# Decode attention on one core: the PE's attention as one 8-round loop, with fixed DMA slots and the output projection behind all of PV

## The chip, the cores and the metric

One core of one Trainium2 chip. The metric is device microseconds of one execution; the spans in the profiles are about 1.8 us shorter than these times (429.7 against 431.48 us in the kernel before), because they begin and end with the kernel's own instructions. The engines go by the profile's names: PE for the matrix products (PEld for its weight loads), DVE, ACT and POOL for the other arithmetic, and SP, which issues the DMAs. QK and PV are the two products of attention, of the queries with K and of the softmax weights with V. Ratios are computed as the mean time of one kernel's fast runs over that of the other's fast runs of the same rounds, so they are not quite the ratio of the medians that are quoted.

## The reference, cut to what matters

Two tokens (batch 2, one query position each) pass through a modulated layernorm, grouped attention over a cache of 32,768 keys, an output projection, and an MLP.

```python
B, Sq, D = (2, 1, 1024)
Hq, Hkv, Sk, Dh = (32, 4, 32768, 128)      # 8 query heads share one K/V head
mod = (_silu(c) @ w_mod)                    # 12.6 MB of weights
h = _layernorm(x) * (1 + ca) + sa
q = h @ wq                                  # 8.4 MB
p = softmax(q @ k_cache^T * Dh**-0.5)       # 67 MB of K
o = p @ v_cache                             # 67 MB of V
x = x + ga * (o @ wo)                       # 8.4 MB
x = x + gb * MLP(modulated layernorm(x))    # w1, w2: 14.7 MB
```

In all 178 MB are read once, for a few matrix products with two columns. There are 2 x 4 = 8 pairs of batch and K/V head; one pair is called a round below. A round reads 4 chunks of K and 4 chunks of V of 2 MB each.

## The kernel before

Everything large goes through one SBUF arena of 160 KB per partition, by DMAs that the SP issues in the order of a list, each as soon as the PE has released the bytes that it overwrites. Before, the arena is a ring of any item sizes, so ten 2 MB chunks fit.

```python
KT_sb = [sb(f"KT_sb{i}", [128, 8, 128], BF16) for i in range(NKT)]     # NKT = 6
arena = nc.alloc_sbuf_tensor("arena", [128, RING], mybir.dt.uint8)     # RING = 160 * 1024
abase = nc.lookup_mloc(arena).addr
...
for n in range(NK + VLAG):                          # NK = 32 chunks, VLAG = 5
    if n < NK:
        add(("K", n), [TPC, D], kv_src(A_k_cache, n // NCH, n % NCH))
    v = n - VLAG
    if v >= 0:
        add(("V", v), [TPC, D], kv_src(A_v_cache, v // NCH, v % NCH))
        if v % (2 * NCH) == 2 * NCH - 1:            # after every second round
            add(("wo", g), [8, DM], ...)
```

The PE transposes a K chunk in 8 groups of 8 tiles, the DVE and the ACT copy the transposed tiles to SBUF, the PE multiplies them with the 8 query columns, and, a softmax later, it multiplies the weights with V. All of this is straight-line code: each of the 8 rounds is written out, and each wait compares a semaphore with a constant.

```python
for n in range(NK + VLAG + 1):
    for g8 in range(TPC // 8):
        if n < NK:
            ...                                      # 8 transposes, one copy of 128x1024
            pipe.append((n, g8, kn))
        if pipe and (len(pipe) > PIPE or n >= NK):
            qk(*pipe.pop(0))                         # 8 matmuls of 8 columns
        for fn in later.get((n, g8), ()):            # softmax, extract, wo
            fn()
    if 0 <= n - VLAG < NK:
        pv(n - VLAG)                                 # 16 matmuls of 512 columns
```

## Time and profile before

| | before |
|---|---|
| time, median of 3 runs | 431.48 us (431.33 to 431.48) |
| span in the profile | 429.7 us |
| data packets (queue q1), share of 16 DMA engines' span | 97.6% |
| instruction packets (queue q8) | 47 of 16 KB, 0.6% |
| PE busy | 292.2 us (68%) |
| duration of a 16 KB data packet, read from the trace's DMA records | 611 ns |

The first lines are from the page of the kernel before: busy time by engine, the bytes a second in 40 slices of the span, the DMA queues (packets, MB, share of 16 engines' span), the shares of the chain that ended last, and two lines of the DMA issues (count, KB each, median us to landing).

```profile
PE 292.2 (68%) x6035; PEld 258.2 (60%) x6035; DVE 162.5 (38%) x344; ACT 158.9 (37%) x266; POOL 1.3 (0%) x9
...
GB/s 332 432 422 426 433 432 424 432 424 427 427 432 427 426 433 429 427 433 426 426 432 426 430 433 424 429 432 426 429 429 428 430 429 424 435 424 424 427 386 112
...
q1 hardware_dynamic: 14112, 178.27, 97.6%
q8 instruction: 47, 0.77, 0.6%
...
DMA 70%; PE 24%; ACT 2%; DVE 2%; issue 1%; SPq 1%; ACTq 0%
...
K<-in_A_k_cache_dram SPq DMA_DIRECT2D x32, 2048.0 KB, 44.2
V<-in_A_v_cache_dram SPq DMA_DIRECT2D x32, 2048.0 KB, 43.2
```

The DMA is the limit: nothing dips between the first slice and the last two (422 to 435 GB/s), and a chunk lands 44 us after its issue, which is about the time that nine others ahead of it in the queue take (9 x 2.1 MB at 428 GB/s, an estimate). The PE is off the critical path for most of the run (24% of the chain, the DMA 70%). But q8 is worth a look: the page lists packets of the program itself among those of the DMA engines, 47 of them, and in the trace's DMA records 46 of the 47 overlap a data packet that takes over 150 ns longer than others of its size.

The second view is the table by stretches of the same kernel, for the last 14 us. Its columns are the stretch, its length, busy us (and instructions) of PE, weight load, DVE, ACT and POOL, the granted clock (as a share of the PE's full clock), the DMA share, and GB/s.

```profile
412.00:414.00 2.00, 0.76 (x28) 0.77 (x29) 0.22 (x1) 0.00 (x0) 0.00 (x0) 0.50 1.02 426
...
416.00:418.00 2.00, 0.00 (x0) 0.00 (x0) 0.00 (x0) 0.00 (x0) 0.00 (x0) 0.50 0.76 315
418.00:420.00 2.00, 1.84 (x64) 1.79 (x64) 0.00 (x0) 0.00 (x0) 0.00 (x0) 0.50 0.51 209
420.00:422.00 2.00, 0.03 (x2) 0.00 (x0) 0.00 (x0) 0.00 (x0) 0.00 (x0) 0.50 0.52 221
422.00:424.00 2.00, 0.69 (x26) 0.70 (x27) 0.00 (x0) 0.00 (x0) 0.00 (x0) 0.50 0.46 193
424.00:426.00 2.00, 1.44 (x55) 1.36 (x52) 0.00 (x0) 0.00 (x0) 0.00 (x0) 0.50 0.21 78
```

The reader should look at the DMA share. It falls to one half at about 417 us and stays there for 6 us, the half-busy tail below: eight of the sixteen engines, by that share, have nothing left to do (the trace's DMA records have 16 data packets under way at 414 us and 8 at 420 us), while the other eight still carry pieces of the last weights, for which the kernel must wait (the chain's last DMA, of `w`, lands at 425.7 us).

Third, the PE's timeline at about 75 us, where the PE has data and no wait (start, us, engine, line, operation; in brackets the idle time before and its cause):

```profile
74.97 0.24 PE L441 MATMUL psS<-qT,KT_sb 128*128 128x8 bf16 x4
76.08 0.26 PE L441 MATMUL psS<-qT,KT_sb 128*128 128x8 bf16 x4 [0.87 <-issue]
```

The PE stands still for 0.87 us in the middle of eight equal matmuls, for nothing that the profile shows. The trace's DMA records have an instruction packet that starts at 73.8 us and takes 0.88 us. Such packets come about once per 256 PE instructions (47 for 12,070 matmuls and weight loads); the 256 instructions of one packet are called a page below.

### The profile page before, as it was taken

Reading aid. Unit: us, or ns where it says so; the run is one execution under the profiler, and the core shown is the slowest. Engines: PE = TensorE matmul, PEld = TensorE weight load, DVE = VectorE, ACT = ScalarE, POOL = GpSimd, SP = SyncE. Lnnn points to the kernel's source line nnn. Section 1 sums busy time; section 2 is a strip of 40 time slices with the busy share of each in tenths; the row PEclk is TensorE's granted clock in tenths of the full one; section 3 lists DMA queues with packets and bytes.
Section 4 is the critical chain, followed back from the end, with each engine's and each line's share of the span. In section 5 each row is a group of like instructions: output and inputs, shape, how many; then the busy total and the mean of one; then the engine's idle time right before and its main releaser. Section 6 shows DMA issues by size and latency. Waiting matters only on the chain.

```text
span 429.7 us, 12974 instructions
## 1 busy us (share of the span) xinstructions
PE 292.2 (68%) x6035; PEld 258.2 (60%) x6035; DVE 162.5 (38%) x344; ACT 158.9 (37%) x266; POOL 1.3 (0%) x9
## 2 busy tenths in 40 slices
PE   0643379859978764997877649777777697535553
PEld 0632379858867663896757548667666585203543
DVE  0200027545665332463543435445434454203200
ACT  1100016575574325362833534446436343500100
POOL 1000000000000000000000000000000000000000
PEclk9999999998989867696996959986988599555555
DMA  8999999999999999999999999999999999999992
GB/s 332 432 422 426 433 432 424 432 424 427 427 432 427 426 433 429 427 433 426 426 432 426 430 433 424 429 432 426 429 429 428 430 429 424 435 424 424 427 386 112
DMA packets 14500, 179.11 MB, mean 417 GB/s; under 512 B 1767, under 2 KB 1774, under 8 KB 2798
## 3 DMA queue, kind: packets, MB, share of 16 engines
q1 hardware_dynamic: 14112, 178.27, 97.6%
q8 instruction: 47, 0.77, 0.6%
q10 hardware_dynamic: 334, 0.02, 0.1%
q14 instruction: 7, 0.06, 0.0%
HBM read 178.28 MB, written 0.00 MB: 415 GB/s over the span
## 4 chain that ended last, share of the span: by engine, by line
DMA 70%; PE 24%; ACT 2%; DVE 2%; issue 1%; SPq 1%; ACTq 0%
DMA K<-in_A_k_cache_dram 50%; PE psKT L546 15%; DMA V<-in_A_v_cache_dram 9%; DMA w<-in_B_w_dram 7%; DMA wmod<-in_w_mod_dram 5%; PE psS L441 4%; PE psO L473 2%; PE psM L510 1%; ACT E_sb L462 1%; SPq L344 1%; PE psM L494 0%; DVE KT_sb L552 0%; PE psM L483 0%; ACT L462 0%; DVE msum L488 0%
## 5 line engine op out<-in xcount | busy, mean ns | idle before, releaser
L546 PE MATMUL psKT<-ident,K 128*128 128x128 bf16 x2048 | 181.1, 240 | 55.1 <-DMA K<-in_A_k_cache_dram 54.2
L546 PEld LDWEIGHTS psKT<-ident,K 128*128 128x128 bf16 x2048 | 138.2, 108 | 70.0 <-DMA K<-in_A_k_cache_dram 63.5
L550 ACT ACTIVATE KT_sb<-psKT 128x1024 bf16<-128x1024 bf16 x96 | 98.3, 1024 | 190.2 <-PE psKT L546 181.3
L552 DVE COPY KT_sb<-psKT 128x1024 bf16<-128x1024 bf16 x160 | 108.2, 689 | 137.7 <-PE psKT L546 137.0
L441 PE MATMUL psS<-qT,KT_sb 128*128 128x8 bf16 x2048 | 91.6, 168 | 7.2 <-ACT KT_sb L550 4.5
L441 PEld LDWEIGHTS psS<-qT,KT_sb 128*128 128x128 bf16 x2048 | 84.0, 100 | 8.6 <-ACT KT_sb L550 4.9
L473 PE MATMUL psO<-V,E_sb 128*32 128x512 bf16 x512 | 38.2, 424 | 10.1 <-DMA V<-in_A_v_cache_dram 9.5
L462 ACT ACTIVATE E_sb<-S_sb,negm 128x256 bf16<-128x256 f32 x64 | 32.5, 508 | 7.0 <-DVE negm L460 5.2
L447 DVE TENSOR_REDUCE m1c<-S_sb 128x8 f32<-128x512 f32 x32 | 22.0, 688 | 14.1 <-ACT S_sb L446 13.0
L473 PEld LDWEIGHTS psO<-V,E_sb 128*32 128x32 bf16 x512 | 11.5, 101 | 22.3 <-DMA V<-in_A_v_cache_dram 13.3
L446 ACT ACTIVATE S_sb<-psS 128x512 f32<-128x512 f32 x32 | 19.0, 594 | 4.4 <-PE psS L441 4.3
L418 PE MATMUL psS<-siluT,wmod 128*128 128x2 bf16 x384 | 11.2, 165 | 8.4 <-DMA wmod<-in_w_mod_dram 6.9
L418 PEld LDWEIGHTS psS<-siluT,wmod 128*128 128x128 bf16 x384 | 10.9, 104 | 8.8 <-DMA wmod<-in_w_mod_dram 7.3
L426 PE MATMUL psS<-hT,wq 128*128 128x2 bf16 x256 | 7.5, 165 | 12.5 <-DMA wq<-in_A_wq_dram 12.5
L426 PEld LDWEIGHTS psS<-hT,wq 128*128 128x128 bf16 x256 | 7.1, 104 | 12.8 <-DMA wq<-in_A_wq_dram 12.8
L591 PE MATMUL psS<-gT,w 128*128 128x2 bf16 x224 | 6.6, 165 | 9.2 <-DMA w<-in_B_w_dram 9.2
L395 ACT ACTIVATE stat<-stat 128x2 f32<-128x2 f32 x3 | 0.6, 203 | 31.8 <-DVE stat L394 31.8
L591 PEld LDWEIGHTS psS<-gT,w 128*128 128x128 bf16 x224 | 6.3, 104 | 9.5 <-DMA w<-in_B_w_dram 9.5
L462 ACT ACTIVATION_READ_ACCUMULATOR E_sb<-S_sb,negm 128x1 f32 x64 | 12.0, 187 | 0.0
L485 DVE RECIPROCAL rinv<-psM 128x1 f32<-128x1 f32 x8 | 1.3, 168 | 22.1 <-PE psM L483 22.1
L573 PE MATMUL psS<-h2T,w 128*128 128x2 bf16 x224 | 7.8, 172 | 2.5 <-DVE x1b L577 1.3
L573 PEld LDWEIGHTS psS<-h2T,w 128*128 128x128 bf16 x224 | 7.6, 118 | 2.6 <-issue 2.6
(86 smaller groups left out, 93.3 us busy)
## 6 DMA issues: line engine op xcount, KB each, us to landing
K<-in_A_k_cache_dram SPq DMA_DIRECT2D x32, 2048.0 KB, 44.2
V<-in_A_v_cache_dram SPq DMA_DIRECT2D x32, 2048.0 KB, 43.2
wmod<-in_w_mod_dram SPq DMA_DIRECT2D x8, 1536.0 KB, 17.2
wq<-in_A_wq_dram SPq DMA_DIRECT2D x4, 2048.0 KB, 37.7
wo<-in_A_wo_dram SPq DMA_DIRECT2D x4, 2048.0 KB, 43.0
w<-in_B_w_dram SPq DMA_DIRECT2D x4, 1792.0 KB, 41.8
w<-in_B_w_dram SPq DMA_DIRECT2D x3, 2048.0 KB, 31.0
w<-in_B_w_dram SPq DMA_DIRECT2D x1, 1024.0 KB, 29.4
```

The costliest lines, as they stand in the source:

```text
L418: pe(lambda e, w=it.view, j=j, k=k: e.matmul(psS[0][:, 2 * j:2 * j + 2], lhsT=w[:, j * 128:(j + 1) * 128], rhs=siluT[:, :, k], start=(k == ...
L426: pe(lambda e, w=it.view, h=h, k=k: e.matmul(psS[1][:, 2 * h:2 * h + 2], lhsT=w[:, k % 2, h * 128:(h + 1) * 128], rhs=hT[:, k, :], start=( ...
L441: pe(lambda e, t=t, jj=jj: e.matmul(ps[:, t * HPG:(t + 1) * HPG], lhsT=KT_sb[kn][:, jj, :], rhs=qT[:, b, g * HPG:(g + 1) * HPG], start=Tru ...
L446: act(lambda e: e.activation(Sc, ps[:, :].rearrange("p (t h) -> p h t", h=HPG), ACT.Copy), reads=[preg], writes=[f"S_sb{i % 2}_{cc}"])
L447: dve(lambda e: e.tensor_reduce(m1c[:, :, cc], Sc, AX.X, ALU.max), reads=[f"S_sb{i % 2}_{cc}"], writes=[f"m1c{cc}"])
L462: act(lambda e, h=h: e.activation(E_sb[j][:, :, h, :], S_sb[j][:, h, :].rearrange("p (u t) -> p u t", t=4), ACT.Exp, bias=negm[j][:, h:h + ...
L473: pe(lambda e, t4=t4, tg=tg, q=q: e.matmul(psO[32 * q:32 * q + 32, :], lhsT=E_sb[j][:, tg // 4, :, :].rearrange("p h t -> p (h t)"), rhs=i ...
L546: pe(lambda e, kq=kq, jj=jj, w=it.view, t=t: e.transpose(psKT[kq][:, jj * 128:(jj + 1) * 128], w[:, t, :], ident[:, :]), reads=[it.reg, "i ...
L550: act(lambda e, kn=kn, src=src: e.activation(KT_sb[kn][:, :, :], src, ACT.Copy), reads=[f"psKT{kq}"], writes=[f"KT_sb{kn}"])
L552: dve(lambda e, kn=kn, src=src: e.tensor_copy(KT_sb[kn][:, :, :], src), reads=[f"psKT{kq}"], writes=[f"KT_sb{kn}"])
L573: pe(lambda e, w=it.view, fc=fc, q=q, j=j, k=k: e.matmul(psS[0][:, 2 * fc:2 * fc + 2], lhsT=w[:, k % 2, q * 512 + j:(q + 1) * 512:4], rhs= ...
L591: pe(lambda e, w=it.view, q=q, j=j, k=k: e.matmul(psS[1][:, 2 * k:2 * k + 2], lhsT=w[:, q % 2, j * DM + k * 128:j * DM + (k + 1) * 128], r ...
```

## The change

The intent: the 8 rounds become one loop on the PE, whose body is about 1,200 instructions (256 transposes, 256 QK and 64 PV matmuls, each with its weight load, are 1,152; the rest are small matmuls, branches and register operations). For that, every K and V chunk gets a fixed slot (8 slots of 16 KB instead of a ring), each producer gets a semaphore of its own that counts rounds, and the PE's waits compare with a register. The other engines' code stays straight-line. The query columns of a round are copied by the POOL to one place, E_sb and two small tiles exist once instead of twice, the copies of K have 8 buffers instead of 6, and the output projection of all four groups moves behind the last PV. The core of the diff, cut:

```diff
-VLAG = 5
-NKT = 6
+NKT = 8
...
+    def _loop(self, eng, body, bounds):
+        with eng.Fori(*bounds) as it:
+            val = {(1, 0): it}
+            for scale, off in ((1, -1), (16, 0), (16, -1)):
+                val[scale, off] = eng.snap(it * scale + off * scale)
+            for always, ops in body:
+                ...                                  # the waits: wait_ge(sem, val[scale, off])
+                if always:
+                    run()
+                else:
+                    with eng.If(it > bounds[0]):     # what lags one round behind
+                        run()
...
-    atT = [sb(f"atT{i}", [128, 8, 2], BF16) for i in range(2)]
+    qcur = sb("qcur", [128, HPG], BF16)
+    atT = [sb(f"atT{i}", [128, 8, 2], BF16) for i in range(G)]
-    yacc = sb("yacc", [128, KT8, 2])
...
-    negm = [sb(f"negm{i}", [128, HPG]) for i in range(2)]
-    rowsum = [sb(f"rowsum{i}", [128, HPG]) for i in range(2)]
+    negm = sb("negm", [128, HPG])
+    rowsum = sb("rowsum", [128, HPG])
-    E_sb = [sb(f"E_sb{i}", [128, NT // 4, HPG, 4], BF16) for i in range(2)]
+    E_sb = sb("E_sb", [128, NT // 4, HPG, 4], BF16)
...
+    SLOT = {("K", 0): 0, ("K", 1): 1, ("V", 0): 2, ("V", 1): 3, ("K", 2): 4, ("V", 2): 5, ("K", 3): 6, ("V", 3): 7}
...
+    T.fold(rounds)
...
+    for g in range(G):
+        it = need("wo", g)
+        ...                                          # wo, all four groups, into one PSUM tile
```

## The prediction

> **What bounds the kernel now.** The DMA. The page's slices show the 16 engines 90% busy or more from start to the last slice, at 420 to 435 GB/s, the chain of waits 70% DMA. The PE has slack: when it catches up (75 to 86 us, the timeline) a K chunk takes 6.2 us, or with its PV also 6.2 us, so about 25 us a round, while a round's 16.8 MB need about 39 us of DMA. There is no hole in the DMA until 416 us; then, in the table by stretches, the DMA share falls to 0.5 from 418 to 423 us and to 0.4 until 425; the last landing is at 425.7. Half of the engines end 7 to 8 us before the other half, and the last `w2` pieces wait for these.
>
> **Why half are late.** The page's queue list shows queue q8, kind instruction: 47 packets of 16 KB, 0.6% of 16 engines' span. The packets' times in the trace are spread over the whole run, about one for each 256 PE instructions, and their durations (0.88 to 0.97 us) repeat with period 8, so I read 8 of the 16 engines in turn, about 6 each. 7 us over 6 pages is about 1.2 us a page: the late half is late because it feeds the PE its program (estimate). At page ends the PE stops for 0.87 us about 1.4 us after the packet began, so pages are fetched nearly on demand and not far ahead.
>
> **What the change does.** Bytes of data, matmuls, evacuations and exps are the same. The ring shrinks from 10 slots to 8; stream order equals PE order, so 7 slots, about 34 us, stay queued: no DMA hole. Output projection (4 x 1.8 us of PE) moves behind PV, under the landing of wo, w1, w2. The PE's program becomes about 1,300 instructions ahead, a body of about 1,250, and 1,650 behind: 17 pages instead of 47, if the body stays on chip. [...] No loop in this trace decides. [...] I give 70% that the body stays.
>
> - Body stays: 28 to 30 pages fewer, 3.5 to 3.7 per late engine x about 1.2 us = about 4.3 us from the DMA's end, all on the critical path: 427.
> - Body is fetched each round: 50 to 60 pages[...]: 432 to 433.
>
> [...]
>
> **Prediction:** 427.6 us, 8 in 10 between 425.5 and 433. Faster by over 2%: 0.05; within: 0.90; slower: 0.05.
>
> **What would show it.** q8 packets about 17 to 25 (body stays) or 50 and more; the DMA share's half-busy tail 3 to 4 us instead of 8; DMA share 1.0 and GB/s unchanged before; PE busy hardly changed; last landing at about 421.5 us.
>
> **What would make it wrong.** Back edges or Ifs that cost many us and push a round's PE time over 39 us: the K stretches would then wait for the PE and the DMA share fall. A slot that comes free late (8 instead of 10) and leaves DMA holes. The late half late for another reason than pages.

How the number comes about: 431.5 us of the kernel before, less about 4.3 us, is about 427 if the body stays, and 432 to 433 if it is fetched each round; 427.6 lies a little above the first.

## The result, and the profile after

| | before | after |
|---|---|---|
| time, median of 4 runs each | 431.46 us | 430.73 us (430.44 to 430.87) |
| ratio | | 0.9983 (0.9969 to 0.9997) |
| span in the profile | 429.7 us | 429.0 us |
| instruction packets (q8) | 47 | 16 |
| duration of a 16 KB data packet, mean of the undisturbed ones | 611.0 ns | 615.6 ns |
| the same for 8 KB and 7 KB packets | 309.0, 272.0 ns | 314.8, 277.2 ns |

The kernel was to gain about 3.9 us and gained 0.7. The same lines of the page of the kernel after:

```profile
PE 289.7 (68%) x6035; PEld 253.2 (59%) x6035; DVE 162.9 (38%) x340; ACT 155.0 (36%) x266; POOL 2.8 (1%) x17
...
GB/s 330 428 418 418 428 419 429 422 424 425 428 428 428 428 428 425 428 428 428 427 428 428 428 425 429 426 429 425 429 426 427 428 428 427 428 424 412 419 416 155
...
q1 hardware_dynamic: 14112, 178.27, 98.4%
q8 instruction: 16, 0.26, 0.2%
...
DMA 79%; PE 17%; ACT 1%; SPq 1%; DVE 1%; issue 1%; DVEq 0%; ACTq 0%
...
K<-in_A_k_cache_dram SPq DMA_DIRECT2D x32, 2048.0 KB, 32.2
V<-in_A_v_cache_dram SPq DMA_DIRECT2D x32, 2048.0 KB, 35.7
```

And the last stretches:

```profile
416.00:418.00 2.00, 0.35 (x13) 0.36 (x14) 0.00 (x0) 0.00 (x0) 0.00 (x0) 0.50 0.99 410
418.00:420.00 2.00, 1.52 (x57) 1.43 (x54) 0.00 (x0) 0.00 (x0) 0.00 (x0) 0.50 1.03 430
420.00:422.00 2.00, 0.00 (x0) 0.00 (x0) 0.00 (x0) 0.00 (x0) 0.00 (x0) 0.50 0.73 295
422.00:424.00 2.00, 1.38 (x52) 1.39 (x52) 0.00 (x0) 0.00 (x0) 0.00 (x0) 0.50 0.39 156
424.00:426.00 2.00, 1.38 (x51) 1.29 (x47) 0.00 (x0) 0.00 (x0) 0.00 (x0) 0.50 0.01 4
```

Half of what was foreseen is there. The body is not fetched again: after the first round there is no instruction packet from 91.5 to 380 us, 16 are left of 47, and the half-busy tail shrinks from about 8 us to about 3. But the tail did not become shorter by ending earlier. It became shorter because the early half now ends at 420.5 us instead of 416.7. The engines were slower in the mean over the run, and the DMA share shows no gap (1.01 from 80 to 380 us in both): q1's packets take 98.4% of 429.0 us (422.1 us an engine) against 97.6% of 429.7 (419.4), though they carry the same 178.27 MB and are less disturbed (16 instruction packets, not 47). Where no instruction packet comes at all, in slices 11 to 34, the rate is an even 425 to 429 GB/s, no better than before with its packets; outside of the loop, where data packets are 7 to 12 KB, it falls to 412 to 419 in five slices (a sixth of 419, slice 6, already carries 16 KB packets).

The DMA records say how. Most data packets take 3 to 11 ns longer, and about as much at 7 KB as at 16 KB (in the mean 5.2 ns at 7 KB, 5.8 at 8, 3.2 at 12, 4.6 at 16): more like a fixed addition to each packet than one in step with its size. Over the 12,672 large packets, 8,704 x 4.6 + 1,024 x 3.2 + 1,920 x 5.8 + 1,024 x 5.2 ns = 60 us, or 3.7 us for each of 16 engines. That is about the size of what was missing. A fixed addition for each packet points to something that every packet shares, and the sizes, the sources and the queue are the same.

What had changed was the address. The tensors ahead of the arena changed in size: KT_sb by +4,096 bytes a partition, E_sb by -4,096, atT by +64, yacc by -64, negm and rowsum by -32 each, qcur by +32 (16 bytes, rounded up). Together that is -32. When both kernels are built, the arena starts at byte 61440 before and at 61408 after: 61440 is a multiple of 256, 61408 lies 224 past one. That the address is the cause, and that 256 bytes are the step that counts, was the guess, which neither of the two traces showed. It was for the chip to say.

### The profile page after: what moved, and what is told of

Same layout as the page of the kernel before. It is cut to its first block, busy times and chain, and to the rows that moved or that the text cites. A ratio compares the mean times of both kernels' runs of the same rounds, so it can differ in the third digit from the quotient of the medians.

```text
span 429.0 us, 13364 instructions
## 1 busy us (share of the span) xinstructions
PE 289.7 (68%) x6035; PEld 253.2 (59%) x6035; DVE 162.9 (38%) x340; ACT 155.0 (36%) x266; POOL 2.8 (1%) x17
## 3 DMA queue, kind: packets, MB, share of 16 engines
q1 hardware_dynamic: 14112, 178.27, 98.4%
## 4 chain that ended last, share of the span: by engine, by line
DMA 79%; PE 17%; ACT 1%; SPq 1%; DVE 1%; issue 1%; DVEq 0%; ACTq 0%
DMA K<-in_A_k_cache_dram 59%; PE psKT L476 11%; DMA wo<-in_A_wo_dram 8%; DMA w<-in_B_w_dram 7%; DMA wmod<-in_w_mod_dram 5%; PE psS L488 3%; PE psO L518 1%; SPq L373 1%; ACT KT_sb L480 1%; PE psS L612 0%; ACT E_sb L509 0%; PE psO L646 0%; ACT L509 0%; DVE KT_sb L482 0%; PE psM L422 0%
## 5 line engine op out<-in xcount | busy, mean ns | idle before, releaser
L476 PE MATMUL psKT<-ident,K 128*128 128x128 bf16 x2048 | 175.2, 238 | 42.5 <-DMA K<-in_A_k_cache_dram 42.5
L476 PEld LDWEIGHTS psKT<-ident,K 128*128 128x128 bf16 x2048 | 134.3, 106 | 52.8 <-DMA K<-in_A_k_cache_dram 49.3
L488 PE MATMUL psS<-qcur,KT_sb 128*128 128x8 bf16 x2048 | 88.8, 168 | 9.8 <-ACT KT_sb L480 7.1
L488 PEld LDWEIGHTS psS<-qcur,KT_sb 128*128 128x128 bf16 x2048 | 80.1, 99 | 15.5 <-ACT KT_sb L480 9.4
L455 PE MATMUL psO<-hT,wq 128*128 128x2 bf16 x256 | 7.5, 165 | 12.9 <-DMA wq<-in_A_wq_dram 12.9
L612 PE MATMUL psS<-atT,wo 128*128 128x2 bf16 x256 | 7.5, 165 | 12.4 <-DMA wo<-in_A_wo_dram 12.4
L612 PEld LDWEIGHTS psS<-atT,wo 128*128 128x128 bf16 x256 | 7.1, 104 | 13.3 <-DMA wo<-in_A_wo_dram 13.3
L455 PEld LDWEIGHTS psO<-hT,wq 128*128 128x128 bf16 x256 | 7.1, 104 | 13.2 <-DMA wq<-in_A_wq_dram 13.2
L646 PE MATMUL psO<-gT,w 128*128 128x2 bf16 x224 | 6.6, 165 | 9.8 <-DMA w<-in_B_w_dram 9.8
L646 PEld LDWEIGHTS psO<-gT,w 128*128 128x128 bf16 x224 | 6.3, 104 | 10.1 <-DMA w<-in_B_w_dram 10.1
```

Of the source, the lines that this page charges most:

```text
L455: pe(lambda e, w=it.view, h=h, k=k: e.matmul(psO[:, 2 * h:2 * h + 2], lhsT=w[:, k % 2, h * 128:(h + 1) * 128], rhs=hT[:, k, :], start=(k = ...
L476: pe(lambda e, kq=kq, jj=jj, w=it.view, t=t: e.transpose(psKT[kq][:, jj * 128:(jj + 1) * 128], w[:, t, :], ident[:, :]), reads=[it.reg, "i ...
L488: pe(lambda e, t=t, jj=jj: e.matmul(ps[:, t * HPG:(t + 1) * HPG], lhsT=KT_sb[g8][:, jj, :], rhs=qcur[:, :], start=True, stop=True), reads= ...
L612: pe(lambda e, w=it.view, g=g, j=j, k=k: e.matmul(psS[0][:, 2 * k:2 * k + 2], lhsT=w[:, j, k * 128:(k + 1) * 128], rhs=atT[g][:, j, :], st ...
L646: pe(lambda e, w=it.view, q=q, j=j, k=k: e.matmul(psO[:, 2 * k:2 * k + 2], lhsT=w[:, q % 2, j * DM + k * 128:j * DM + (k + 1) * 128], rhs= ...
```

## The experiments

Theory A: two effects of equal size cancel, a gain from 31 instruction packets fewer and a loss from the arena's address. Rival B: the loop gains little, because the DMA's rate falls for another reason (8 slots, another order of the stream, another core). Theory A has two halves, which the first three runs take apart. All runs gave correct results. Unless said otherwise, one set of runs shares the kernel before on its chip: 431.39 us in the first set, of which one run of 538.6 us is left out.

### The kernel after, with the arena back on its old address

```diff
+    sb("pad", [128, 8])
     arena = nc.alloc_sbuf_tensor("arena", [128, RING], mybir.dt.uint8)
```

> The kernel after, with 32 bytes of padding ahead of the DMA arena, so that it starts at byte 61440 of each partition as before, and not at 61408 (224 past a multiple of 256). Theory A (the start address): 16 KB data packets go back from 612 to 621 ns to a flat 611, 8 KB ones from 313 to 320 to 309; about 12,700 packets over 16 engines at 4 to 6 ns each are 3.9 us an engine, so 426.8 us (426 to 427.8), last landing at about 421. Rival B (the order of the stream, 8 slots in place of 10, or the core that was profiled): nothing changes, 430.7 us and packets of 612 to 621 ns. Instruction packets: 16 in both.

Measured: 426.17 us (425.94 to 426.33), ratio to before 0.9879 (0.9864 to 0.9895), 16 instruction packets, 16 KB packets of 611.0 ns, 8 KB 309.0. The last stretches:

```profile
414.00:416.00 2.00, 0.99 (x38) 0.91 (x35) 0.00 (x0) 0.00 (x0) 0.00 (x0) 0.50 1.03 434
416.00:418.00 2.00, 0.00 (x0) 0.00 (x0) 0.00 (x0) 0.00 (x0) 0.00 (x0) 0.50 0.73 299
418.00:420.00 2.00, 1.87 (x64) 1.79 (x64) 0.00 (x0) 0.00 (x0) 0.00 (x0) 0.50 0.33 139
420.00:422.00 2.00, 1.02 (x33) 0.94 (x33) 0.41 (x2) 0.00 (x0) 0.00 (x0) 0.50 0.04 8
```

Here the early half ends where it did before (the share drops in 416 to 418), and the late half ends 5 to 6 us earlier than before. Three stretches of the middle make the same point; they are of the kernel before, the kernel after and this one, in this order:

```profile
20.00:40.00 20.00, 8.21 (x279) 7.73 (x276) 0.78 (x4) 0.00 (x0) 0.00 (x0) 1.00 1.01 425
80.00:380.00 300.00, 227.29 (x4397) 198.77 (x4393) 137.51 (x265) 142.24 (x245) 0.00 (x0) 0.84 1.01 428
```

```profile
20.00:40.00 20.00, 7.96 (x269) 7.48 (x267) 0.78 (x4) 0.00 (x0) 0.00 (x0) 1.00 1.01 418
80.00:380.00 300.00, 228.08 (x4366) 193.98 (x4363) 141.78 (x271) 140.12 (x247) 1.32 (x7) 0.87 1.01 427
```

```profile
20.00:40.00 20.00, 8.27 (x281) 7.79 (x279) 0.78 (x4) 0.00 (x0) 0.00 (x0) 1.00 1.01 426
80.00:380.00 300.00, 232.01 (x4423) 198.57 (x4419) 141.81 (x271) 139.69 (x247) 1.33 (x7) 0.85 1.01 431
```

With a DMA share of 1.01 in all six, the DMA was never idle; only its rate differs. 32 bytes of padding are worth 4.6 us. Rival B falls, its slower core included: the arena at 61504, below, ran on the same chip as this one and took 429.92 us.

### The kernel before, with the arena moved off its address

```diff
+    sb("pad", [128, 120])        # 480 bytes: the arena starts at 61920, 224 past a multiple of 256
     arena = nc.alloc_sbuf_tensor("arena", [128, RING], mybir.dt.uint8)
```

> The kernel before, with the arena moved by 480 bytes to 61920 (224 past a multiple of 256, as after). Theory A: packets of 612 to 621 ns, 47 instruction packets as before, both delays add up: 431.4 + 3.9 = about 435.3 us (434 to 436.5). Rival B: 431.4 us and packets of 611 ns.

Measured: 436.23 us (436.15 to 436.25), ratio 1.0113 (1.0097 to 1.0129); 47 instruction packets, 16 KB packets of 615.6 ns, 8 KB of 314.8, the very means of the kernel after. The address costs 4.8 us in the kernel before as well, a little more than expected. So it has nothing to do with the loop, the slots or the order. The sum of 3.7 us over the data packets does not give all of the 4.6 to 4.8. A part may be that the instruction packets take longer too: 1.07 us in the mean here and 1.06 in the kernel after, against 0.94 in both aligned kernels, which for 47 packets on 8 engines is 0.75 us (estimate). The rest stays open.

### The aligned kernel after, with its rounds written out

```diff
     sb("pad", [128, 8])
...
-        self.ops["pe"].append(("loop", [], body, (first, max(rounds) + 1)))
+        for it in sorted(rounds):
+            for always, ops in rounds[it]:
+                self.ops["pe"].extend(ops)
```

> The aligned kernel after with its 8 rounds written out again for the PE (same slots, semaphores, order of the stream, output projection behind PV; no loop, no If, waits on constants). If the gain of the loop is the instruction packets that are not fetched: 46 to 48 such packets, half-busy tail of 7 to 8 us again, 431.4 us (430.7 to 432.2), as the kernel before. If slots, order or the projection matter by themselves: a time apart from 431.4 with 47 packets. If packets of instructions cost nothing: the time of the aligned loop.

Measured: 431.55 us (431.34 to 431.60), ratio 1.0003 (0.9989 to 1.0018). 47 instruction packets, and the half-busy tail is back:

```profile
416.00:418.00 2.00, 0.00 (x0) 0.00 (x0) 0.00 (x0) 0.00 (x0) 0.00 (x0) 0.50 0.71 291
418.00:420.00 2.00, 1.52 (x57) 1.52 (x58) 0.00 (x0) 0.00 (x0) 0.00 (x0) 0.50 0.60 254
420.00:422.00 2.00, 0.34 (x13) 0.26 (x10) 0.00 (x0) 0.00 (x0) 0.00 (x0) 0.50 0.47 201
422.00:424.00 2.00, 0.62 (x23) 0.63 (x24) 0.00 (x0) 0.00 (x0) 0.00 (x0) 0.50 0.54 217
424.00:426.00 2.00, 1.42 (x53) 1.33 (x51) 0.00 (x0) 0.00 (x0) 0.00 (x0) 0.50 0.18 74
```

So fixed slots, 8 in place of 10, the new order, the projection behind PV, the semaphores and the padding together are worth nothing, for better or worse: 431.55 against 431.39. All of the gain is in the loop. The four corners:

| | arena on a multiple of 256 | arena 224 past one |
|---|---|---|
| rounds written out, 47 instruction packets | 431.4 (before), 431.55 (after, unrolled) | 436.23 (before, moved) |
| rounds in a loop, 16 instruction packets | 426.17 | 430.73 (after) |

The loop gains 5.4 us on the left (5.2 counted from the kernel before) and 5.5 on the right; the address costs 4.6 to 4.8.

### How round the address has to be

The kernel after with the arena at 61504 (64 past a multiple of 256), at 61568 (128 past), and at 61696 (a multiple of 256, not of 512). The edit is the size of the pad: 24, 40 and 72 elements instead of 8.

> The kernel after with the arena at 61504: a multiple of 64 but 64 past a multiple of 256. If a start off a multiple of 256 is what costs[...]: packets of 612 to 621 ns and 430.7 us still. If a multiple of 64 is enough: 611 ns and 426.8 us.

> The loop with the arena at 61568, 128 past a multiple of 256. If only multiples of 256 are free of the extra time: 16 KB packets of about 614 to 615 ns and about 430 us, as at 64 past. If 128 is enough: 611 ns and 426.2 us.

> The loop with the arena at 61696, a multiple of 256 but not of 512 or 4096. If a multiple of 256 is what the data packets need: 611 ns for 16 KB and 426.2 us. If only a coarser boundary (512, 4096) helps: longer packets and 429 to 431 us.

| start past a multiple of 256 | 16 KB packet, mean | time | median of before in the same set |
|---|---|---|---|
| 0 (61440) | 611.0 ns | 426.17 | 431.39 |
| 0 (61696) | 611.0 ns | 426.05 | 431.32 |
| 64 (61504) | 614.7 ns | 429.92 | 431.39 |
| 128 (61568) | 614.6 ns | 429.77 | 431.43 |
| 224 (61408) | 615.6 ns | 430.73 | 431.46 |

In these five places, a multiple of 256 is enough, and neither 64 nor 128 past one is. The price at 224 past (615.6 ns, 430.73 us) is a little higher than at 64 and 128 (614.7 and 614.6 ns, 429.92 and 429.77 us).

### Does the body really stay, and in how much room?

Two rounds in one body of the aligned loop: 4 iterations of about 2,400 instructions. (The first case of the expectation supposes that the room for the body is smaller than this one.)

```diff
-        with eng.Fori(*bounds) as it:
+        with eng.Fori(1, 5) as it:
+            for half in range(2):                  # round 2 * it - 1 + half
...
-                    with eng.If(it > bounds[0]):
+                        with eng.If(it > 1):        # in the first half alone
```

> The aligned loop with two rounds in one body: 4 iterations of about 2,520 PE instructions, 9.8 pages of 256[...]. If the loop gains because its body stays on chip[...]: every iteration fetches its body again, about 50 instruction packets and 431 to 432.5 us, as without a loop. If the room is larger or the loop gains for another reason (fewer waits, registers): about 21 packets and 427 us.

Measured: 432.64 us (432.62 to 432.94), ratio 1.0033 (1.002 to 1.0046), 53 instruction packets, spread evenly over all four iterations:

```profile
q8 instruction: 53, 0.87, 0.7%
```

A loop with a body of about 4.7 pages of 256 instructions fetched it once (no packet from 91.5 to 380 us in the kernel after); one of twice that size fetched it anew in every iteration (53 packets), and was slower than no loop at all (432.64 against 431.55 us). So it isn't the loop that gains, it is that the body is not fetched again. What differs between the two is the size of the body, so the room for it should lie between about 4.7 and 9.4 pages (an estimate from these two runs); where in between was not shown.

### What one page costs: two misses and a clean dose

To see a page's price apart from the loop, two runs added PE instructions without data. First, the unrolled aligned kernel with every QK matmul issued twice:

```diff
-        for jj in range(8):
+        for k in range(16):
+            jj = k % 8
```

> The unrolled aligned kernel with every QK matmul issued twice (same values to the same place): 4,096 more PE instructions, 16 more pages, no more data; about 6 us more PE work a round, which fits into the PE's slack of about 14 us. If an instruction page costs one of 8 DMA engines about 1.45 us of data time: 63 packets, two more on each of 8 engines, 431.5 + 2.9 = 434.4 us (433.5 to 435.3), with a half-busy tail of about 11 us. If pages are harmless and the loop gains otherwise: 431.5.

Measured: 452.06 us (451.04 to 455.87), ratio 1.0492. There were 63 packets as foreseen, but the PE became the limit: the slices of its page fall to 215 GB/s in places, where the DMA waits for slots. The time says nothing of a page's price. It does say that my slack was wrong: I had taken 25 us of PE work a round from a stretch at full clock, where the PE was behind (75 to 86 us, granted clock 1.00). In the steady part, 100 to 300 us, the PE of the kernel before is busy 156.4 us of 200 at a granted clock of 0.84. That leaves 22% of a round of 39 us, or 8.6 us (not 14). The doubled run asked for more: its PE was busy 344.8 us against 290.2 in the unrolled kernel, 6.8 us more a round, and its QK matmuls stood still for no visible cause for 27.9 us in all against 1.3, 3.3 us more a round; that makes 10.1 us.

Second, the aligned loop with 1,024 idle matmuls where the PE waits for weights:

```diff
+    def more(n):
+        for _ in range(n):
+            T.raw("pe", lambda e: e.matmul(psS[1][:, 0:2], lhsT=ident[:, :], rhs=ident[:, 0:2], start=True, stop=True))
...
+        more(64)        # after each wmod piece; 32 after each half of a wq piece, 64 after each wo piece
```

> The aligned loop with 1,024 idle matmuls of 2 columns (8 pages of instructions, no data) put where the PE waits for weights: 64 after each wmod piece, 32 after each half of a wq piece, 64 after each wo piece. This is the dose that the run with doubled QK was to give, without its load on the PE in the rounds. If a page costs one of 8 DMA engines about 1.43 us of data time: 24 packets, one more on each of 8 engines, 426.2 + 1.4 = 427.6 us (427.0 to 428.2). If pages are harmless and the loop gains otherwise: 426.2.

Measured: 437.26 us (435.80 to 439.38), ratio 1.0145. 24 packets as foreseen, but again the PE, not the DMA: it came 20 us late to the first K chunk, all slots were full, and the DMA lost about 6 us (a share of 0.75 over the 25 us from 75 us on). With 1.4 us for the packets, that is not all of the 9.6 us that the profiled execution took more (435.80 against 426.17); the rest is not accounted for. The chain of waits of this run shows why (start, us, what):

```profile
24.31 1.28 PE psS L452 x48
25.59 1.71 PE psS L447 x64
27.30 0.11 PE psS L452 x4
27.41 2.64 issue
30.05 1.31 PE psS L452 x44
31.36 1.71 PE psS L447 x64
33.06 0.53 PE psS L452 x20
33.60 2.65 issue
```

"issue" is time without a visible wait. It returns after every 128 matmuls (256 instructions: each has its weight load) and lasts 2.3 to 2.9 us; the instruction packets stand in the trace at 21.6, 27.9 and 34.0 us, within about 0.5 us after a stop begins. So with these short matmuls (48 in 1.28 us) the PE stands still at each page's end, and only then does a packet of instructions start. In the kernel before the stop at 75 us was only 0.87 us long, and the packet (73.8 us) began 1.4 us before it; why it came earlier there was not shown.

The clean dose leaves the work alone and loops half of the rounds: 1 to 4 in the loop, 5 to 8 written out.

```diff
-    T.fold(rounds)
+    T.fold({it: rounds[it] for it in (1, 2, 3, 4)})
+    for it in (5, 6, 7, 8):
+        for always, ops in rounds[it]:
+            T.ops["pe"].extend(ops)
```

> The aligned kernel with rounds 1 to 4 in the loop and rounds 5 to 8 written out: the same data and the same PE work, but about 20 instruction pages more than the full loop (16) and some 11 fewer than without a loop (47). The two kernels with doubled QK and with idle matmuls loaded the PE too much to give a clean dose; this one adds no work. If pages are what costs, the time lies on the line through 16 pages (426.1) and 47 pages (431.5), 0.175 us a page: 36 packets and 429.6 us (429.0 to 430.2). If the loop as such saves (or costs) time: half of the difference at the most by chance, and not in step with the packets.

Measured: 429.81 us (429.67 to 430.10), ratio 0.9963 (0.995 to 0.9977), 34 instruction packets:

```profile
q8 instruction: 34, 0.56, 0.5%
```

The kernels whose arena starts on a multiple of 256 and whose PE work is the same:

| instruction packets | 16 | 34 | 47 | 53 |
|---|---|---|---|---|
| time, us | 426.17, 426.05 | 429.81 | 431.4, 431.55 | 432.64 |

From 16 to 53 that is 6.5 us over 37 packets, 0.176 us a packet. If 8 engines share them, a packet costs its engine 1.4 us. The point at 34 lies 0.5 us above the straight line (429.3). Whole packets fit it better: taken in turn by 8 engines, 16, 34, 47 and 53 packets give the busiest engine 2, 5, 6 and 7, and at 1.3 us each the last three would take 3.9, 5.2 and 6.5 us more than the first, where 3.7, 5.3 and 6.5 were measured (estimate, fitted afterwards and not tested by itself). The DMA records give the same sum in another way: an instruction packet takes 0.945 us in the mean, and in the kernel before 46 of the 8,704 data packets of 16 KB, about one for each, take 1.09 us instead of 0.61; 0.945 + 0.48 = 1.43 us.

## Why the prediction was right or wrong

The prediction was 427.6 us, a gain of 3.9 us; the measured gain was 0.7. The time lies in the stated range, but the gain is a fifth of the one foreseen. That the range holds it is luck: the range was wide because it covered two cases, 427 with the body staying and 432 to 433 with it fetched each round. The first case came true, and 430.73 belongs to neither.

- **The DMA is the limit, and the half-busy tail comes from instruction pages.** Right. Unrolled or looped, the tail follows the packets (47: about 8 us; 16: about 3 us), and with 16, 34, 47 and 53 packets the time follows them too.
- **The body stays on chip (70%).** Right, as far as the runs show it, which is that the body is not fetched again: 16 packets against "17 to 25".
- **What 31 packets fewer are worth.** Somewhat low: 4.3 us was expected, 5.4 measured. The late half was about 8.5 us late, not 7, and a page costs 1.4 us, not 1.2.
- **No DMA hole from 8 slots, projection off the path.** Right: the unrolled kernel with all of that takes 431.55 us, before 431.39.
- **"Bytes of data, matmuls, evacuations and exps are the same", and "GB/s unchanged before".** This is the step that failed. The bytes were the same, their rate was not: 427 GB/s from 80 to 380 us, where the same loop reaches 431 with the arena on its old address, and 418 against 426 from 20 to 40 us. I took a data packet's duration as given and did not ask where it lands. The term left out of the sum is the address: +4.6 us. With the terms as measured, -5.4 + 4.6 = -0.8 us, against -0.7 measured. That sum closes almost by construction, as its runs share their ends; the independent check is the kernel before with its arena moved, 431.4 + 4.6 = 436.0 against 436.23 measured.
- **PE slack of 14 us a round** (39 us less 25). Wrong, 8.6 us; it did no harm in the change itself, as the unrolled and the looped kernel do the same PE work in it, but it spoiled an experiment.

The shown best version is the kernel after with 32 bytes of padding: 426.17 us, 1.2% faster than before. What stays open: why, with the arena off a multiple of 256, some packets pay 3 ns and others 10; about 1 us of the address's 4.6 to 4.8, which the data packets do not sum to; and which 8 engines serve the instructions. That there are eight of them is inferred from the half-busy share (0.49 to 0.52 from 418 to 423 us in the kernel before), from the eight data packets under way at 420 us, and from the instruction packets' durations, which repeat with period 8 (mostly 0.88 to 0.97 us).

## What to carry to other kernels

When the DMA is the limit, two things that no data-flow diagram shows belong to the sum: the instructions that the same DMA engines bring (here 0.176 us per 256 PE instructions, to be saved by a loop whose body is fetched once, as about 1,200 instructions were here and about 2,400 were not), and the start address of what the DMA writes. In a kernel like this one, set the address of a DMA buffer explicitly to a multiple of 256 bytes (here 16 KB packets took 611.0 ns at two such starts, 614.6 to 615.6 at three others) instead of leaving it to the sum of the tensors ahead of it: here edits of other tensors, -32 bytes in all, cost 1%. When a clear gain seems to vanish, compare the duration of single packets before asking about waits: a change of a few nanoseconds on every packet hardly shows elsewhere (here as 427 GB/s instead of 431).
